# Attention to 32 memories and a spatial gate on one core: loads, written orders and the last output tile are rearranged

## The chip, the cores and the metric

The kernel runs on 1 core of one Trainium2 chip. The metric is the device time of one execution in microseconds (us). The kernel before was run three times; its time is the median of these.

## What is computed

There are 8 batches, 8 heads, 576 tokens (S), 64 columns per head (D), 32 memories (m), model width 512 and hidden width 1024. The reference, cut to what matters:

```
a     = softmax(phi, over tokens)              # 8 x 8 x 576 x 32
k_m   = einsum('bhsm,bhsd->bhmd', a, k);  v_m likewise from v
attn  = softmax(q @ k_m.T / sqrt(64))          # 576 x 32 per head
x     = attn @ v_m, heads side by side         # 576 x 512 per batch
h     = relu(x @ w_in);  u, v = halves of h    # 576 x 512 each
v_n   = (v - mean) / sqrt(var + 1e-6)          # over the 512 columns
v_s   = w_spatial @ v_n + b_spatial            # mixes the 576 tokens
out   = (u * v_s) @ w_out
```

w_in and w_out lie in memory as 64-bit floats, everything else as 32-bit floats.

## The kernel before

One core does the eight batches one after the other, in stages that overlap. x itself is never formed: the kernel multiplies the 32 memories of each head by w_in first (M = v_m @ w_in, the tiles `mh` and `ml`) and applies the attention weights (`ah`, `al`) to that. Matmuls on large tiles take a pair of rounded values, a high part (`mh`, `ah`, `vh`, `wth`, `gh`) and a low part (`ml`, `al`, `vl`, `wtl`, `gl`), and three products per pair. A low part is made by DVE (the vector engine, line 174), or by a matmul with minus the identity on PE (the matmul engine, line 162) and a copy on ACT (the scalar engine, line 172); the table `ON_VECTOR` says which.

Nothing is left to a scheduler. Each stage is a generator whose `yield`s cut it into steps, and every engine (PE, DVE, ACT, POOL, and SP, which issues all DMAs) executes its instructions in the order in which the written tokens call the steps. `START` is the order of the weights and of batch 0, `PLAN` that of each of the batches 1 to 6, `LAST` that of batch 7. A token is a letter, a number where the stage has several tiles, and one prime for each batch that the step is ahead; `*3` repeats it. The letters:

- Q: load q (batch 0 in one DMA, `q_all`, line 407; other batches in four DMAs of 128-byte pieces, `q_sb`, line 433) and transpose it (line 416 on PE, 442 on DVE).
- P: softmax weights over tokens. Load phi (303), maxima over rows (`half`, `mx`, 292 to 298), transpose on PE (`mt`, 311), maximum (`cm`, 314), spread (`cmb`, 317; `mb`, 320), subtract (322), exp (329), sums (`es`, again 292 to 298).
- K: load k and v (336), memories on PE (`kvm`, 348, 360), divide (`kmn`, 375; `vmn`, 384), transpose (388, 393; `kT`, 397).
- S: scores (460 for batch 0), their softmax (474 to 497) and its transpose `ta` (506) split into `ah`, `al` (509, 511). M: products with w_in (`mp`, 595), split into `mh` (604) and `ml`.
- V: the gate half of h by tiles of 128 tokens (`pv`, 627; bn at 651, normalize at 666, split at 669, 671). U: the other half (`pu`, 693). G: the mix over tokens (`ps`, 731) times u (`g`, 742), split (753, 755). O: the output product (`po`, 771), copied by ACT (777) and stored (780).
- D, E, L: two half loads of w_in (184, each 128 x 1024 words of 4 bytes) per token pair and their decoding to 32-bit floats (193, 195, 199, then the win step, 201). X: the same for w_out. W, T, B: load of w_spatial and of the bias (245 to 248), transposes (`wt`, 261, copied to `wth`, 272), bias row (282, the wsub step 284). Z: a matmul on the identity whose result nobody reads (`idle`, 791).

SP issues DMAs in the same order, and a DMA whose queue is full or whose tile is in use holds what stands behind it on SP. PSUM holds four single banks (`bank`) and two double ones (`banks`).

Of the kernel before, what the change touches and what calls it, by code (L numbers as in the profile page):

```python
# [23 lines left out]


START = """
    Q Z Q*3 Z P Q P*4 K Q P Q*2 P*2 K P Z P*6 K D1*2 K Z E0 K*3 D1 K Q*2 K D1 E1 E0 E1 P' Z K*2 W
    D0 P' S D0 Q S P' K Z E1 S T2 P' S E0 D0 T0 T2 Z S*3 T2 T0 S T0 D0 E0 T2 L0 E1 S*2 M1 T1 P' S
    T0 P' S B P' M1*2 T3 L1 S K' P' M1 L0 M1 K' S*2 P'*2 S T3 S M1 T3 S Q' S Q' S P' Z L1 S M1 K'
    S L0 L1 V0 T1 P' L0 V2 V0 V2 L1 T3 T1 V0 P' V0 M0 B M0 P'*2 V0 V2 K' T1 M0*2 T4 K' P'' V0 K'*2  # L30
    V0 T4 U2 Q' M0 K' Q' V2 X1 M0*2 V1 X1 V1 V3 T4*2 K' V2 V1 K' V2 V3 Q' U2 K' U2 K' X0*2 V3 P''
    U1*2 V1*2 U1 V2 P'' V3 U0 V1 X1 U0 P'' S U3 P'' U3 Q' U0 V4 U3 P'' V1 X1 P'' V4 S'*2 M0'*2 M1'
    S' G0 S'*2 G1*2 V4 S' M0' X0 M0' G1 V3 V4*2 V3 G0 X0 V3 P'' V4*2 P'' V4 G1 M1' X0 G0*2 M1' S'
    X1 G1 X0 G2*2 G0 X1 G3 M0' G3 X0 X1 X0 P'' M0' X1 G1 M1' S' G0*2 G1 G2*2 G0 M1' G0 G3 P'' G1
    Q'' G1 G3 O2 Q'' G3 M0' G2*2 O3 O1 S' K'' G3 G2 G3 M1' S'*2 M1' O3 S'*2 O1 O2 S' O2 O0 G2 O0
    K'' S'*2 G3 S' P'' S'*2 V1' O1 Q'' O0 G3 O0 O2 P'' O3 P'' G2 P'' V1' O1 O3 V1'*2
"""

PLAN = """
    Q' V4 U2 V1 K'*2 U0 Q' V0 K' V4 U3 U0 V0 U3 Q' P'' V2 V0 U1 U3 U1 K' V2 V0 V2 V3 K'*2 Q'' P''  # L40
    S' U1 S'*2 K' M0' V3 V4*2 M1' G0 V3*2 V2 M0' G1 M1' S'*2 M0' S' M1' G1 V2 V3 P'' Q'' G0 M1'
    P'' V2 M0' V4 G0 P'' M0' G1 V3*2 P'' G1 S' M0' G1 G0 P'' G0 S' G1 G2 G1*2 S' K''*2 G0 G1 G0 S'
    G2 S'*2 P'' G2 G0 P'' G3 G0 M1' G3 G2 S' G3 M1' G3 M0' O1 G3 O3 G2 S' P'' M1' O0 G3 P'' G2*2
    G3 S' O1 S' P'' O1 S' G2 S'*2 P'' O0 U2' O3 G3 Q'' O0 K''*2 O0 G2 V4' V1' G3 O4 O3 V4' O4 P'''
    U2' V1'*2 V0' O4 O3 V1' K'' V4' U0' O4 V0'*2 O2 V1' O1 V1' O2*2 P''' V2' O2
"""
# [12 lines left out]

# [812 lines left out]
```

## Time and profile before

| | |
|---|---|
| median of 3 runs | 415.53 us (414.77 to 415.92) |
| profiled execution, its own time | 414.95 us |
| its span, first to last instruction | 413.2 us |
| PE busy | 397.9 us (96%) |
| DVE busy | 283.7 us (69%) |
| ACT busy | 227.2 us (55%) |
| chain that ended last | PE 88%, DVE 4%, DMA 3%, ACT 2%, issue 2% |
| mean granted PE clock | 0.992 of full speed |

Busy time is summed over the span. The chain is followed back from the last instruction, at each step to what released it. Rows of the trace give a start, a duration, engine and line, the tiles as out<-in, and in brackets how long the engine idled before and what ended that; `x4` counts instructions in one row. Lines are those of the kernel before; in the changed kernel they are 3 higher up to the output copy and 7 higher behind it.

### The profile page before, as it was taken

What the parts mean: (1) busy time and instruction counts of PE and PEld (TensorE: products, weight loads), DVE (VectorE), ACT (ScalarE), POOL (GpSimd) and SP (SyncE); (2) the same over time, 40 slices, a digit from 0 to 9 for tenths busy, and PEclk for the clock granted to TensorE, in tenths of its full rate; (3) what the DMA queues carried; (4) which work ended last, traced back from release to release, by engine and by line L of the source; (5) the groups of instructions that cost most, each with busy time, mean ns of one, the idle gap of its engine ahead of it and who ended that gap; (6) DMA issues with size and microseconds to landing.
All of it is one profiled execution on the core that took longest, in us unless ns stands there. A gap on an engine that the chain in (4) does not pass through costs nothing.

```text
span 413.2 us, 9463 instructions
## 1 busy us (share of the span) xinstructions
PE 397.9 (96%) x3963; PEld 337.1 (82%) x3963; DVE 283.7 (69%) x542; ACT 227.2 (55%) x423; POOL 49.0 (12%) x131
## 2 busy tenths in 40 slices
PE   5778999999999999999999999999999999999996
PEld 3444688989798889989798888989798889989984
...
GB/s 293 387 379 252 96 239 254 51 42 132 252 81 27 135 144 230 0 52 154 290 12 25 135 143 229 0 68 137 248 54 37 68 27 1 2 76 27 0 2 127
DMA packets 85790, 50.70 MB, mean 123 GB/s; under 512 B 66226, under 2 KB 70322, under 8 KB 85748
## 3 DMA queue, kind: packets, MB, share of 16 engines
...
q8 instruction: 31, 0.51, 0.5%
...
## 4 chain that ended last, share of the span: by engine, by line
PE 88%; DVE 4%; DMA 3%; ACT 2%; issue 2%; SPq 0%; ACTq 0%; DVEq 0%
PE ps L731 28%; PE po L771 24%; PE pu L693 12%; PE pv L627 10%; PE kvm L348 4%; PE mp L595 2%; DMA w_rem<-in_moe_w_spatial_dram 2%; PE sc L529 2%; DMA q_all<-in_q_dram 1%; PE pv L636 1%; PE idle L791 1%; PE pv L637 1%; PE wt L261 1%; PE tq L416 1%; DVE win_sb L201 1%
## 5 line engine op out<-in xcount | busy, mean ns | idle before, releaser
L731 PE MATMUL ps<-wth,vh 128*128 128x288 f32 x256 | 56.9, 303 | 0.0
L731 PE MATMUL ps<-wth,vl 128*128 128x288 f32 x256 | 55.1, 297 | 0.0
L731 PE MATMUL ps<-wtl,vh 128*128 128x288 f32 x256 | 54.5, 294 | 0.0
L771 PE MATMUL po<-woh,gl 128*128 128x512 f32 x128 | 50.4, 394 | 0.0
L771 PE MATMUL po<-wol,gh 128*128 128x512 f32 x128 | 50.2, 392 | 0.0
L656 POOL TENSOR_SCALAR rs<-mv 128x1 f32<-128x1 f32 (+1 forms) x40 | 11.6, 290 | 324.9 <-DVE den L370 152.7
L771 PE MATMUL po<-woh,gh 128*128 128x512 f32 x128 | 50.0, 391 | 0.0
L651 DVE BATCH_NORM_STATS2 st<-vr 128x6 f32<-128x512 f32 (+1 forms) x40 | 27.0, 676 | 32.3 <-ACT vr L632 31.6
L731 PEld LDWEIGHTS ps<-wth,vh 128*128 128x128 f32 x256 | 41.2, 190 | 6.0 <-PE mp L595 5.9
L777 ACT COPY o<-po 128x512 f32<-128x512 f32 x36 | 20.8, 585 | 45.6 <-PE po L771 43.9
L731 PEld LDWEIGHTS ps<-wth,vl 128*128 128x128 f32 x256 | 41.0, 188 | 0.3 <-DVE vl L671 0.3
L731 PEld LDWEIGHTS ps<-wtl,vh 128*128 128x128 f32 x256 | 41.1, 188 | 0.0
L666 ACT ACTIVATE vr<-vr,sh,rs 128x512 f32<-128x512 f32 (+1 forms) x40 | 32.6, 817 | 4.6 <-POOL sh L661 3.8
L742 DVE TENSOR_TENSOR g<-u,ps 128x576 f32<-128x576 f32 x32 | 23.4, 747 | 10.8 <-PE ps L731 10.7
L771 PEld LDWEIGHTS po<-woh,gl 128*128 128x128 f32 x128 | 24.1, 188 | 5.3
L753 ACT CAST gh<-g 128x512 fp32r<-128x512 f32 x32 | 19.1, 617 | 16.7 <-DVE g L742 16.6
L671 DVE TENSOR_TENSOR vl<-vr,vh 128x512 fp32r<-128x512 f32 x32 | 21.6, 674 | 9.2 <-ACT vh L669 9.2
L771 PEld LDWEIGHTS po<-wol,gh 128*128 128x128 f32 x128 | 24.0, 188 | 4.7
L771 PEld LDWEIGHTS po<-woh,gh 128*128 128x128 f32 x128 | 24.0, 188 | 4.5
L693 PE MATMUL pu<-ah,mh 128*128 128x288 f32 x128 | 27.6, 297 | 0.0
L693 PE MATMUL pu<-al,mh 128*128 128x288 f32 x128 | 27.4, 296 | 0.0
L693 PE MATMUL pu<-ah,ml 128*128 128x288 f32 x128 | 27.3, 294 | 0.0
...
## 6 DMA issues: line engine op xcount, KB each, us to landing
...
```

The lines of the kernel that those rows point to most:

```text
L348: nc.tensor.matmul(kvm[r][32 * j : 32 * j + 32], phi_sb[halves[r], j, i, :], kv_sb[halves[r], j, :, i * D : (i + 1) * D], start=(i == 0), ...
L627: nc.tensor.matmul(pv, x[:, r, cs], m[:, r, DM:DFF], start=(n == 0), stop=(n == 5))
L651: nc.vector.bn_stats(st6, vr)
L656: nc.gpsimd.tensor_scalar_add(rs, mv[:, 1:2], 1e-6)
L666: nc.scalar.activation(vr, vr, AF.Identity, bias=sh, scale=rs)
L671: nc.vector.tensor_tensor(vl[:, st, :], vr, vh[:, st, :].bitcast(F32), op=ALU.subtract)
L693: nc.tensor.matmul(pu[:, hf, 0:HALF], m[:, r, cs], a[:, r, hf * HALF : (hf + 1) * HALF], start=(n == 0), stop=(n == 5),)
L731: nc.tensor.matmul(ps[:, hf, 0:HALF], a, w[:, hf * HALF : (hf + 1) * HALF], start=(n == 0), stop=(n == len(ops) - 1),)
L742: nc.vector.tensor_tensor(g.rearrange("p (a s) -> p a s", a=2), u[:, dt, :].rearrange("p (a s) -> p a s", a=2), ps[:, :, 0:HALF], op=ALU.mult,
L753: nc.scalar.copy(hi, x)
L771: nc.tensor.matmul(po, a, w, start=(n == 0), stop=(n == 11))
L777: nc.scalar.copy(o, po)
```

## The change

All three written orders are new. The parts of it that have a name:

- phi of batch 0 is loaded ahead of q (`P Q P` opens `START`).
- Five half loads of w_in, not four, are issued ahead of phi of batch 1; the other three follow w_spatial.
- q of batch 1 is split around v: k, two q loads, v, two q loads. One half of w_out is loaded ahead of phi of batch 2.
- There are seven idle matmuls, not eight.
- `ON_VECTOR` names other low parts: the counts (six `ml`, two `wtl`) are the same.
- The last output tile, now that of O3, is copied in two halves, by ACT and by DVE.

The diff, with the orders cut to their first lines:

```
 START = """
-    Q Z Q*3 Z P Q P*4 K Q P Q*2 P*2 K P Z P*6 K D1*2 K Z E0 K*3 D1 K Q*2 K D1 E1 E0 E1 P' Z K*2 W
-    D0 P' S D0 Q S P' K Z E1 S T2 P' S E0 D0 T0 T2 Z S*3 T2 T0 S T0 D0 E0 T2 L0 E1 S*2 M1 T1 P' S
...
+    P Q P Z P K*2 D1 P Q P*2 Q*2 P*2 Q P*3 Q P Z P Q D1 Q K E0 D1*2 P*2 K*2 Z K*2 E0 K Q*2 K E1
+    K*2 E0 Q D0 E1*2 K P' E0 Z S P'*2 S W S P' S Z S D0 Z P' T0 T2 S T0 P' S*2 D0 E1 T0 T2 D0 P'
...
 LAST = """
...
-    O1 O3 G2 O0 G2 O3 G3 O1 G3 O0*2 O4 O2 O4 O3 O1 O2*2 O3 O4 O2
...
+    G3*3 O1*3 G3 O2 O0 O2 G0 O4 O1 G3 O4 O0 O4 O0 O4 O3*3 O2 O3
 """
+
+FINAL = int(LAST.split()[-1][1])
...
-    E0 E1 L0 L1 X0 X0.sign X1 X1.sign ml001 ml011 ml100 ml101 ml110 ml111 wtl1 wtl4
+    E0 E1 L0 L1 X0 X0.sign X1 X1.sign ml000 ml001 ml010 ml101 ml110 ml111 wtl3 wtl4
...
         o = four.tile([P, DM], F32, name="o")
-        nc.scalar.copy(o, po)
+        if b == B - 1 and st == FINAL:
+            nc.scalar.copy(o[:, 0:256], po[:, 0:256])
+            nc.vector.tensor_copy(o[:, 256:DM], po[:, 256:DM])
+        else:
+            nc.scalar.copy(o, po)
```

What it moves on the engines, at three places. First SP, the DMA queue's engine, from the first loads of w_in (`raw`) to q of batch 1; the rows above these are phi, q, k and v of batch 0. Before:

```order
L184 DMA raw<-in_moe_w_in_dram 128x1024 x4
L303 DMA phi_sb<-in_phi_dram 128x4x288
L245 DMA w_sb<-in_moe_w_spatial_dram 128x4x576
L246 DMA w_rem<-in_moe_w_spatial_dram 64x576
L248 DMA b_sb<-in_moe_b_spatial_dram 1x576 x2
L184 DMA raw<-in_moe_w_in_dram 128x1024 x4
L336 DMA kv_sb<-in_k_dram 128x4x576
L336 DMA kv_sb<-in_v_dram 128x4x576
L433 DMA q_sb<-in_q_dram 32x72x32 x4
```

Changed:

```order
L187 DMA raw<-in_moe_w_in_dram 128x1024 x5
L306 DMA phi_sb<-in_phi_dram 128x4x288
L248 DMA w_sb<-in_moe_w_spatial_dram 128x4x576
L249 DMA w_rem<-in_moe_w_spatial_dram 64x576
L251 DMA b_sb<-in_moe_b_spatial_dram 1x576 x2
L187 DMA raw<-in_moe_w_in_dram 128x1024 x3
L339 DMA kv_sb<-in_k_dram 128x4x576
L436 DMA q_sb<-in_q_dram 32x72x32 x2
L339 DMA kv_sb<-in_v_dram 128x4x576
L436 DMA q_sb<-in_q_dram 32x72x32 x2
```

A fifth `raw` precedes phi of batch 1 and all that follows it, and v of batch 1 now stands behind two of the four `q_sb` loads.

Second PE, around the first transposes of w_spatial (`wt`), where it also takes the transpose of the row maxima of batch 1 (`mt`). `mp` is M of batch 0, `ta` the transpose of its attention weights. Before, from the last of the first M products on:

```order
L595 MATMUL mp_1_0_415<-win_sb,vT 32x512
L595 MATMUL mp_1_1_416<-win_sb,vT 32x512
L261 MATMUL wt_425<-ident,w_sb 128x128 x4
L261 MATMUL wt_425<-ident,w_rem 128x64
L311 MATMUL mt_436<-ident,mx 128x128
L162 MATMUL mp_1_0_415<-mh,minus 128x512
L261 MATMUL wt_444<-ident,w_sb 128x128 x4
L261 MATMUL wt_444<-ident,w_rem 128x64
L506 MATMUL ta_459<-ident,sm_all 128x128 x3
L320 MATMUL mb_464<-ident,cmb 128x128
```

Changed, from the idle matmuls ahead of the first `wt` on:

```order
L798 MATMUL idle<-ident 128x512 x2
L264 MATMUL wt_381<-ident,w_sb 128x128 x4
L264 MATMUL wt_381<-ident,w_rem 128x64
L264 MATMUL wt_387<-ident,w_sb 128x128 x4
L264 MATMUL wt_387<-ident,w_rem 128x64
L314 MATMUL mt_395<-ident,mx 128x128
L165 MATMUL wt_381<-wth,minus 128x256
L165 MATMUL wt_381<-wth,minus 128x320
L598 MATMUL mp_1_0_421<-win_sb,vT 32x512
L598 MATMUL mp_1_1_422<-win_sb,vT 32x512
```

`mt` stood behind the low parts of `wth`, the M products and a third `wt`; it now follows the second `wt` at once.

Third, the end of the program with the semaphores that each instruction waits for. SP before:

```order
L780 DMA out_dram<-o 128x512 [waits DMAHW0_49]
L780 DMA out_dram<-o 128x512 [waits DMAHW1_49,Activation_49]
L782 DMA out_dram<-o 64x512 [waits DMAHW2_49]
L783 DMA out_dram<-o 64x512 [waits DMAHW3_49]
L780 DMA out_dram<-o 128x512 [waits DMAHW4_49,Activation_49]
```

SP changed:

```order
L787 DMA out_dram<-o 128x512 [waits DMAHW0_49,Activation_49]
L789 DMA out_dram<-o 64x512 [waits DMAHW1_49,Activation_49]
L790 DMA out_dram<-o 64x512 [waits DMAHW2_49]
L787 DMA out_dram<-o 128x512 [waits DMAHW3_49]
L787 DMA out_dram<-o 128x512 [waits DMAHW4_49,DVE_49]
```

DVE changed, its last instructions (before, it had no part in the output tile):

```order
L745 TENSOR_TENSOR g<-u,ps_3_4894 128x576 [waits DVE_49,PE_49]
L758 TENSOR_TENSOR gl<-g,gh 128x512 [waits Activation_49]
L758 TENSOR_TENSOR grl<-g,grh 128x64
L758 TENSOR_TENSOR grl<-g,grh 128x64 [waits Activation_49]
L782 COPY o<-po_3_5038 128x256 [waits DMAHW4_49,DMAHW3_49,DMAHW7_49,DMAHW0_49,Activation_49]
```

The last store waited for ACT and now waits for DVE, and DVE's half of the copy waits for ACT, not for PE.

## Rows read from the trace of the kernel before

**Rows 1.** The page: busy us of each engine, share of the span, instructions.

```profile
PE 397.9 (96%) x3963; PEld 337.1 (82%) x3963; DVE 283.7 (69%) x542; ACT 227.2 (55%) x423; POOL 49.0 (12%) x131
```

**Rows 2.** Windows: stretch, length, busy PE, PEld, DVE, ACT, POOL, PE clock, DMA share, GB/s.

```profile
20.00:30.00 10.00, 7.31 (x161) 4.73 (x159) 7.57 (x10) 5.75 (x10) 0.00 (x0) 0.87 1.04 380
27.30:34.20 6.90, 6.37 (x28) 2.94 (x29) 4.20 (x8) 4.67 (x8) 0.00 (x0) 0.51 1.04 393
48.00:91.00 43.00, 42.87 (x326) 37.22 (x327) 40.66 (x71) 30.94 (x55) 5.34 (x14) 1.00 0.51 146
50.00:400.00 350.00, 349.93 (x3325) 306.33 (x3326) 251.91 (x488) 194.28 (x371) 44.78 (x116) 1.00 0.37 101
```

**Rows 3.** Timeline, 0 to 20 us: start, us, engine, line, operation, idle before.

```profile
6.27 1.97 PE L416 MATMUL tq<-ident,q_all 128*128 128x128 f32 x8 [2.20 <-DMA q_all<-in_q_dram]
...
7.89 0.69 DVE L292 TENSOR_TENSOR half<-phi_sb 128x512 f32<-128x512 f32 x1 [7.89 <-DMA phi_sb<-in_phi_dram]
...
16.50 1.14 ACT L193 ACTIVATE raw<-raw 128x1024 int32<-128x1024 uint32 x1 [2.11 <-DMA raw<-in_moe_w_in_dram]
...
17.55 0.60 ACT L375 ACTIVATE kmn<-kvm,den 128x128 f32<-128x128 f32 x2
```

**Rows 4.** Timeline, 20 to 30 us.

```profile
20.14 0.35 ACT L397 COPY kT<-tk 128x256 f32<-128x256 f32 x1
...
22.10 0.69 DVE L292 TENSOR_TENSOR half<-phi_sb 128x512 f32<-128x512 f32 x1 [0.60 <-DMA phi_sb<-in_phi_dram]
...
25.56 0.69 DVE L476 TENSOR_TENSOR sm_all<-sc,rmx_all 128x512 f32<-128x512 f32 x1
...
25.64 0.66 PE L261 MATMUL wt<-ident,w_sb 128*128 128x128 f32 x4 [1.45 <-DMA w_sb<-in_moe_w_spatial_dram]
...
26.86 10.57 SPq L433 DMA_DIRECT2D q_sb<-in_q_dram  x2
```

**Rows 5.** Timeline, 30 to 51 us.

```profile
30.05 1.35 DVE L486 TENSOR_REDUCE rsum_all<-sm_all 128x36 f32<-128x1152 f32 x1 [1.54 <-ACT sm_all L483]
...
35.01 0.29 DVE L314 TENSOR_REDUCE cm<-mt 128x2 f32<-128x128 f32 x1 [1.90 <-PE mt L311]
...
41.76 0.90 DVE L511 TENSOR_TENSOR al<-ta,ah 128x384 fp32r<-128x384 f32 x1
...
43.17 2.34 DVE L201 SCALAR_TENSOR_TENSOR win_sb<-raw 128x1024 int32<-128x1024 int32 x2
...
47.79 0.29 DVE L298 TENSOR_TENSOR es<-es,phi_sb 128x128 f32<-128x128 f32 x1
...
49.90 0.53 PE L693 MATMUL pu<-ah,mh 128*128 128x288 f32 x2
```

**Rows 6.** Timeline, 69 to 72 and 89 to 92 us.

```profile
69.83 0.75 DVE L742 TENSOR_TENSOR g<-u,ps 128x576 f32<-128x576 f32 x1
...
90.00 0.76 DVE L574 TENSOR_TENSOR al<-aT,ah 128x576 fp32r<-128x576 f32 x1 [0.17 <-ACT ah L572]
...
90.74 0.39 PE L627 MATMUL pv<-ml,ah 128*128 128x512 f32 x1
...
90.97 0.39 PE L627 MATMUL pv<-mh,al 128*128 128x512 f32 x1
```

**Rows 7.** DVE by line and form, 0 to 60 us: busy us, mean ns.

```profile
L201 DVE SCALAR_TENSOR_TENSOR win_sb<-raw 128x1024 int32<-128x1024 int32 x4 | 4.7, 1212 | 0.0
...
L294 DVE TENSOR_TENSOR half<-half 128x256 f32<-128x256 f32 x5 | 2.1, 417 | 0.1
...
L174 DVE TENSOR_TENSOR ml<-mp,mh 128x512 fp32r<-128x512 f32 x2 | 1.3, 660 | 0.0
...
L284 DVE TENSOR_TENSOR ws<-b_sb,ws 1x576 fp32r<-1x576 f32 x1 | 0.8, 755 | 0.0
```

**Rows 8.** Timeline, the last matmul and the last copy.

```profile
409.05 0.40 PE L771 MATMUL po<-woh,gl 128*128 128x512 f32 x1
409.52 0.58 ACT L777 COPY o<-po 128x512 f32<-128x512 f32 x1 [1.73 <-issue]
```

More of the change, by code (lines that the diff above doesn't have):

```diff
@@ L26 @@
 START = """
-    Q Z Q*3 Z P Q P*4 K Q P Q*2 P*2 K P Z P*6 K D1*2 K Z E0 K*3 D1 K Q*2 K D1 E1 E0 E1 P' Z K*2 W
-    D0 P' S D0 Q S P' K Z E1 S T2 P' S E0 D0 T0 T2 Z S*3 T2 T0 S T0 D0 E0 T2 L0 E1 S*2 M1 T1 P' S
-    T0 P' S B P' M1*2 T3 L1 S K' P' M1 L0 M1 K' S*2 P'*2 S T3 S M1 T3 S Q' S Q' S P' Z L1 S M1 K'
-    S L0 L1 V0 T1 P' L0 V2 V0 V2 L1 T3 T1 V0 P' V0 M0 B M0 P'*2 V0 V2 K' T1 M0*2 T4 K' P'' V0 K'*2
-    V0 T4 U2 Q' M0 K' Q' V2 X1 M0*2 V1 X1 V1 V3 T4*2 K' V2 V1 K' V2 V3 Q' U2 K' U2 K' X0*2 V3 P''
@@ L32 @@
[L32 to L36, printed above, removed]
+    P Q P Z P K*2 D1 P Q P*2 Q*2 P*2 Q P*3 Q P Z P Q D1 Q K E0 D1*2 P*2 K*2 Z K*2 E0 K Q*2 K E1
@@ new lines @@
+    K*2 E0 Q D0 E1*2 K P' E0 Z S P'*2 S W S P' S Z S D0 Z P' T0 T2 S T0 P' S*2 D0 E1 T0 T2 D0 P'
+    S*2 P' S B S M1 P' L0 T0 T2 T1 M1 T2 S L1 S P' M1 S M1 L0 M1 S L1 S*4 T3 K' M1 S T1 L1 S Q' M1
+    Z L0 L1 V2 L0 V2 V0 K' T1 P' V2 M0 P'*2 V0 M0 P' K' M0 P' V2 V0*2 M0 T1 K' M0 T4 Q' X1 T3 V1
+    M0 V2 V0 M0 U2 K' V2 T3 U2 P'' V1 X1 T4 T3 V3 V0 U1 Q'*2 K' V1 X0 T4 X0 S U2 U1 K' T4 V1 K' U3
+    K'*2 B U3 V2 V1 U1 V0 V1 U0*2 Q'*2 P'' V1 V3 K' X1 V3 U3 P'' V4 P'' V3 U0 X1 K' S' V4 S'*2 X0
+    K'' M1' Q'' M0' M1' G0 S'*2 M1' V3 V4 K'' V3 G1 S' M1' G1 V4 P'' G1 V4 M0' G0 M0' V3 P'' G0
@@ L37 @@
+    V4*2 X0 P'' V4 G1 X1 P'' X0 S' G1 M0' X0 X1 G0 X0 M1' G3 G0 X0 M1' X1 P'' G3 X1 G1 G3 M0' G1
+    G3 G0 G2 G1 G0 G2 P'' M0' G0 Q'' G1 M0' G0 G2*2 G3 O2 G2 O3 S' G2 S' G3 G2 P'' G3 O1 S' O3
+    S'*2 O2 G2 S' O2 O3 S' P'' S' P'' O1 O0*2 O1 S' G2 P'' O1 S' G3 M1' G3 U2' S'*2 O3 O0*2 P''
+    V1' Q'' O2 V1'*2 Q'' V1'
 """
 PLAN = """
-    Q' V4 U2 V1 K'*2 U0 Q' V0 K' V4 U3 U0 V0 U3 Q' P'' V2 V0 U1 U3 U1 K' V2 V0 V2 V3 K'*2 Q'' P''
-    S' U1 S'*2 K' M0' V3 V4*2 M1' G0 V3*2 V2 M0' G1 M1' S'*2 M0' S' M1' G1 V2 V3 P'' Q'' G0 M1'
@@ L42 @@
[L42 to L45, printed above, removed]
+    K' V4 V0 U2 V1 P'' U0 V4 Q' U0 Q'' K' U1 K' Q' U1 V0 P'' V2 U3*2 V0 V3 V0 V2 K' U3 K' S' U1 S'
+    K' M1' M0' V2 S'*2 V3 M1' V2 V3*2 V4 G0 V2 G1 S' V3 G0 S' M1' V3 V2 V4 V3 G1 V4 G1 S' M0'
@@ L46 @@
+    P''*2 M0' G1 S' G0*2 G3 G1 M1' M0' P'' Q'' G3 G0 G1 P'' S' G3 M0' M1' G1 G3 P'' M1' P'' M0'
+    K'' S' G1 M1' G2*2 G0 G2 G1 G0 S' G0 O3 S' P'' G2 G0 O1 G3 G2 G3 S' G2 G3 G2 S'*2 O0 M0' S' O1
+    U2' P'' O0 O3 O1 G3 P'' S'*2 P'' S' O0 O3 P''*2 O3 K''*2 V1' K'' O1 V4' V1' G3 V1' V4' O2*2
+    V4' O0 V1' O2 P''' G2 V0'*2 G2 O4 Q'' V1' U2' O4 U0' V0' O4 V1' V2' K''' Q'' O2 O4 K''
 """
 LAST = """
-    U2 V3 V0 V4 V0*2 U0 V2 V1 U1*2 V0 V3 U0 U1 V2 U3*2 V4 G0 V2 G0 G1*2 V2 V3 U3 V1 V2 V4*2 V3*3
@@ L50 @@
-    V2 G1 G0 V4 V3 G1*2 G0 G2 G0 G2 G0 G1 G3 G0 G1 O0 G1 G3 G2 G3*2 G0 G1 G3 G0 G2 O4 G3*2 O1 G2*3
-    O1 O3 G2 O0 G2 O3 G3 O1 G3 O0*2 O4 O2 O4 O3 O1 O2*2 O3 O4 O2
+    U2 V0 V2 V0 V4 V0 U0 V1 U3 U0 U3 V3 V2 U1 V0 U3 V4 U1 V3 V2 G0 V4 U1 V2*2 V4 V3 G0 G1*2 V3 V2
+    V3 V4 G1 G0 V3*2 G0*2 G1 G3 G0 G1 G3 G1 G2 G3 G2 G0 G2 G1*2 O2 G1 G2 O0 G2 G3 G2 V1 G2 G0 G2*2
+    G3*3 O1*3 G3 O2 O0 O2 G0 O4 O1 G3 O4 O0 O4 O0 O4 O3*3 O2 O3
 """
+FINAL = int(LAST.split()[-1][1])
 ON_VECTOR = set(
     """
-    E0 E1 L0 L1 X0 X0.sign X1 X1.sign ml001 ml011 ml100 ml101 ml110 ml111 wtl1 wtl4
+    E0 E1 L0 L1 X0 X0.sign X1 X1.sign ml000 ml001 ml010 ml101 ml110 ml111 wtl3 wtl4
```

## The prediction, made before the change was run

> **What bounds the kernel now.** The busy line of the page comes first [rows 1]: PE, the matmul engine, is busy for 397.9 us of a span of 413.2, so some 15 us are left that an order of work could win at all. The windows say where they lie [rows 2]. From 50 to 400 us PE is busy for 349.93 us of 350: it never waits there. All its gaps lie in the first 50 us and in the last few. In the gapless stretch the change leaves PE the same matmuls, so only three things can move the end: how much work PE has behind it when the gapless stretch begins, whether a new gap opens later, and what follows the last matmul. From 48 to 91 us DVE, the vector engine, is busy for 40.66 us of 43, so DVE decides for batch 0 how early PE's food is ready. The timeline of the first 50 us then shows what DVE itself waits for.
>
> The sum is made against the profiled execution, whose own time is 414.95 us, 1.75 more than its span. The median of the runs is 415.53, so 0.58 is added at the end. A measurement of this kernel can tell some 0.3% from no change, 1.25 us: under 414.3 counts as faster, over 416.8 as slower.
>
> **Part 1, phi ahead of q: nothing.** phi is half as large as q, so it lands first, and the maxima of batch 0 can start some 3 us before 7.89 [rows 3]. But `mt`, which takes their transpose, stands on PE behind the first transpose of q, which waited for q until 6.27 and now waits for both, until about 7.9. What is left of the gain, under 1 us at `kvm`, dies on ACT: the decode of w_in (16.50, ended 2.11 us of idling for its load) still stands ahead of `kmn` (17.55). The bytes ahead of the first half load of w_in are the same in sum, so the decode and `kmn` stay where they are. Bounds: 0 to 0.9 gained; I take 0, since the row of `kmn` follows the decode's at once.
>
> **Part 2, the fifth half load ahead of phi of batch 1: DVE is ahead by 2.0 us after it.** One half load is 128 x 1024 words of 4 bytes, 0.52 MB. The transfers are saturated here (380 GB/s from 20 to 30 us, DMA share 1.04 [rows 2]), so all that is queued behind it lands 0.52 MB / 380 GB/s = 1.4 us later: phi of batch 1 at 23.5 instead of 22.1, w_sb at 27.0 instead of 25.6 [rows 4]. The new DVE order puts the win step of the decoded half into the hole ahead of phi, then takes the same maxima. By the durations of the rows the last score subtraction ends at 28.15 (it was 25.56 + 0.69 = 26.25). So DVE is 1.9 us late there. This is the price.
>
> What it buys comes next. Of the two win steps behind the subtractions (1.21 us each [rows 7]) one is now done in that hole, and the other fills time in which DVE used to idle: `rsum` waited 1.54 us for the exponentials [rows 5]. Then the order pays: `cm` waited 1.90 us for `mt` on PE, because `mt` stood behind the low parts of `wth`, the first M products at half clock and another weight transpose. Now it stands ahead of all of these and `cm` is done before `rsum`, at 29.6 against 30.05: 0.45 us early. From there the steps up to the third `al` are the same but for the lost wait, for `cm` itself (0.29) and for the last maximum (put at 0.29, as the `es` step of its shape), which lie behind: 0.45 + 1.90 + 0.29 + 0.29 = 2.9 early, `al` ends at 39.8 instead of 42.66. The wins, the gate's bn and the `es` sums follow; the wsub step (0.755 [rows 7]) is moved behind them, so `es` ends 2.9 + 0.76 - 0.16 = 3.5 us early, at 44.6 (it was 48.08). The 0.16 is a wait that my walk puts at the bn behind the gate's relu. PE, which waits on just these tiles, begins its gapless stretch (`pu` at 49.90 [rows 5]) early by as much.
>
> **Part 3, what batch 0 takes back: 1.5 us of 3.5.** DVE has no slack from here to 91 us, so each step that the new order puts earlier on it costs its duration. Up to the first `g` (69.83 [rows 6]) these are wsub, 0.755, and one more low part of M of batch 1, 0.66 [rows 7]: 3.5 - 1.42 = 2.1. Up to the last `al` of batch 1 (90.00, for which the sixth matmul of `pv` at 90.97 is just in time) they are wsub, one `half` of 128 x 256 (0.417), one sum (0.29) and two `grl` of 128 x 64, put at 0.2 each by the 0.29 of 128 x 128: 3.5 - 1.86 = 1.6; but there PE has done half a u tile more, six matmuls of 288 columns at 288/512 of the 0.23 us between the starts of the two `pv` of 512 [rows 6], 0.8 us: 2.4. The smaller decides: about 2.0 us gained. I read PE's own side as the check: its list up to the first `pu` is as long, less one idle matmul. A loose walk, in which each releaser costs what it cost before, gives 2.1 there.
>
> Bounds: at most 3.0 (all of `al`'s lead is kept), at least 0.
>
> **Part 4, the low parts on DVE or on PE: nothing of its own.** Six `ml` and two `wtl` are on DVE before and now; only which ones. One low part of batch 0 leaves PE and one of batch 1 goes there: each is one matmul of 512 columns, so PE's sum is the same.
>
> **Part 5, the order of batches 1 to 7: nothing.** PE's matmuls are equal and it has no gap to lose [rows 2]. I set DVE's work against PE's need, token by token, with the durations of the rows: the least slack in a body is 3.1 us before, 5.0 after. On SP the stores of out and the q loads now stand ahead of v, but v is issued some 14 us ahead of its use. Batch 7 has some 0.2 us of slack at the last gate tile and at the last `g`, as before. Cover that fails there costs what is late, 1 us or so.
>
> **Part 6, the last tile in two halves: +0.2.** Before, one ACT copy of 512 columns (0.58) stands between the last matmul and the store [rows 8]. In the built order the DVE half waits for ACT, and the last store for DVE: the halves run one after the other. ACT's copy of 256 columns took 0.35 (`kT` [rows 4]), the nearest DVE step on 128 x 256 takes 0.417 [rows 7]: 0.77 without a pause between them, so +0.2. The bound on the other side, both at once, is 0.42 - 0.58 = -0.2. No row shows two engines reading one bank together. The Trainium skill, "PSUM — Partial Sum Buffer", section "PSUM bank collisions raise a hardware error", says that two engines may not access one bank in the same partitions at the same time, disjoint columns included; by that rule a split by columns can only be serial, as the built order has it, and splitting costs instead of saving.
>
> **The sum:** -2.0 + 0.2 = -1.8: 413.15 for the profiled execution, **413.7** on the median.
>
> **The rivals.**
> - *B, a new wait eats the lead.* The v load of batch 1 was issued ahead of the q loads; now two of these stand ahead of it, and SP was held for 10.57 us by the first two [rows 4]. v is then issued near 26.9 + 10.6 = 37.5 or later, and its 1152 KB at 380 GB/s land from about 41.2; the `kvm` that reads them comes at about 43.5 in my walk, behind the first gate tiles that need the third `al`. That is 2.3 us of slack in an estimate which is off by as much. If it fails, the lead of 2.0 goes first: 415.5 and no measurable change. The DMA share of 1.04 and 1.04 in the windows from 20 to 34 us speaks for it; the share of 0.51 from 48 us on [rows 2] says that the queue runs empty soon after, against.
> - *C, the clock (the slower side).* PE ran at half its clock, 0.51 granted in the window of 27.3 to 34.2 us, with 6.37 us busy of 6.9 [rows 2]; from 20 to 30 us it was busy for 7.31 us of ten. It cost 0.5 x 6.9 = 3.4 us of PE's time, most of it under DVE's cover. The new order has an emptier PE ahead of w_sb's transposes, 1.4 us longer. If the fall comes 10 us later, in the dense stretch, nothing covers it: 413.7 + 3.4 = 417.1. It decides from the point where the low stretch begins after about 40 us. Against it: the mean clock of 50 to 400 us is 1.00, so a PE that works without gaps did not lose it once.
> - *D, the whole lead is kept,* since PE does other work where DVE repays: -3.0 + 0.2, 412.7; without the serial tail 412.3.
>
> The Trainium skill, "TensorE: Matmul & The Clock Gate", section "HAM oscillation — how this bites in real kernels", says that a wait for DMA lets the clock fall and that the next dense part then starts slow; the fall at 27.3, behind 1.45 us of waiting for w_sb [rows 4], agrees. By it alone the fall stays with that wait, ahead of the dense stretch, and C would get half its chance.
>
> **How the numbers follow.** Forecast A, 413.7, 0.48; its own range is 412.9 to 414.4. B, 415.5 (414.3 to 416.7), 0.25. C, 417.1, 0.14. D, 412.5, 0.13. Faster: nearly all of A (0.44) and D, 0.56. Same: the rest of A and nearly all of B, 0.28. Slower: C and a little of B, 0.16. The range takes in D's centre and B whole: 412.0 to 416.9 leaves out a tenth or so on the slow side and a few hundredths on the fast one.
>
> **What would show it.** phi and w_sb of batch 1 land 1.4 us later; `cm` no longer waits for `mt`; `es` of batch 1 ends near 44.6; the first `pu` starts 2 to 3 us before 49.9; at the first `g` some 2 us are left, and they last to the end; behind the last matmul two copies stand one after the other, 0.8 us. Wrong: a `kvm` of batch 1 that ends its wait on v; a low clock after 40 us; PE under 349 of 350 us from 50 to 400; a lead that is there at 50 us and gone at 91.

## The result, and the profile after

| | before | changed |
|---|---|---|
| median of 4 runs | 415.26 us | 410.85 us (409.96 to 411.28) |
| ratio, 95% interval | | 0.9903 (0.9882 to 0.9923) |
| span of the profiled execution | 413.2 us | 408.8 us |
| mean granted PE clock of it | 0.992 | 0.994 |

The change makes the kernel faster by 4.4 us, where 1.8 had been forecast, and the time lies under the range given. The 415.26 are four runs; 80 later runs of the kernel before, beside the experiments, have a median of 414.7, against which the change gains 3.9. The busy line of the page of the changed kernel, against [rows 1]:

```profile
PE 392.5 (96%) x3961; PEld 335.0 (82%) x3961; DVE 287.9 (70%) x543; ACT 229.9 (56%) x423; POOL 47.6 (12%) x131
```

PE is busy for 5.4 us less with the same matmuls but for one idle step, which is two of them. Part of this is clock, as the windows of the changed kernel show (columns as in [rows 2]):

```profile
28.50:31.70 3.20, 3.20 (x22) 1.23 (x22) 2.56 (x5) 2.98 (x6) 0.00 (x0) 0.50 1.04 390
50.00:400.00 350.00, 350.00 (x3331) 306.60 (x3330) 252.79 (x483) 196.17 (x369) 42.87 (x114) 1.00 0.36 98
```

The stretch at the lower level, 1.2 GHz, is a little over 3.2 us here and was 6.9 [rows 2]; from 50 to 400 us PE is as full as before, by its busy time. The timeline of the changed kernel tells the steps up to the gapless stretch (columns as in [rows 3]):

```profile
13.84 2.22 PE L351 MATMUL kvm<-kv_sb,phi_sb 64*32 64x128 f32 x143 [1.21 <-DMA kv_sb<-in_v_dram]
...
22.73 0.69 DVE L295 TENSOR_TENSOR half<-phi_sb 128x512 f32<-128x512 f32 x1 [0.21 <-DMA phi_sb<-in_phi_dram]
...
26.38 0.69 DVE L479 TENSOR_TENSOR sm_all<-sc,rmx_all 128x512 f32<-128x512 f32 x1
...
26.55 0.66 PE L264 MATMUL wt<-ident,w_sb 128*128 128x128 f32 x4 [1.40 <-DMA w_sb<-in_moe_w_spatial_dram]
...
29.04 0.29 DVE L317 TENSOR_REDUCE cm<-mt 128x2 f32<-128x128 f32 x1 [0.84 <-PE mt L314]
29.25 1.34 DVE L489 TENSOR_REDUCE rsum_all<-sm_all 128x36 f32<-128x1152 f32 x1
...
37.56 1.65 DVE L514 TENSOR_TENSOR al<-ta,ah 128x384 fp32r<-128x384 f32 x2
...
42.91 2.21 PE L351 MATMUL kvm<-kv_sb,phi_sb 64*32 64x128 f32 x143
...
43.84 0.29 DVE L301 TENSOR_TENSOR es<-es,phi_sb 128x128 f32<-128x128 f32 x1
...
48.57 0.42 PE L696 MATMUL pu<-ah,mh 128*128 128x288 f32 x2 [0.50 <-DVE qT L445]
...
67.45 0.75 DVE L745 TENSOR_TENSOR g<-u,ps 128x576 f32<-128x576 f32 x1
...
87.73 0.76 DVE L577 TENSOR_TENSOR al<-aT,ah 128x576 fp32r<-128x576 f32 x1
...
404.45 0.40 PE L774 MATMUL po<-woh,gl 128*128 128x512 f32 x1
404.93 0.37 ACT L781 COPY o<-po 128x256 f32<-128x256 f32 x1 [2.21 <-PE po L774]
405.33 0.42 DVE L782 COPY o<-po 128x256 f32<-128x256 f32 x1 [7.74 <-ACT o L781]
```

The reader is to hold these against [rows 4 to 6] and [rows 8]. phi and w_sb land later (22.73 against 22.10, 26.55 against 25.64); the wait of `cm` for `mt` falls from 1.90 to 0.84 us and lies ahead of `rsum`; the third `al` ends at 39.21 (37.56 + 1.65) against 42.66, the sums `es` at 44.13 against 48.08. DVE is then 3.95 us ahead, 2.38 at the first `g`, 2.27 at the last `al` of batch 1. But the last matmul starts 4.60 us earlier. So PE won a further stretch of time after 92 us, where by its busy time there was nothing to win.

**A measure of this: the lead.** Each matmul shape gets its usual distance from start to next start (the median over all compared kernels, idle matmuls left out). The lead of a kernel at a time is the work, so counted, that the kernel before has still to start then, less the work that this one has.

| lead over the profiled execution of before, us | 48 | 100 | 205 | 310 | 360 | 400 |
|---|---|---|---|---|---|---|
| changed kernel | 2.97 | 2.78 | 3.54 | 4.12 | 4.45 | 4.58 |

2.8 us are there at 100 us, 1.8 more come in the bodies of batches 1 to 7, and from the start of the last `po` the changed kernel takes 4.37 us where before took 4.12: 2.8 + 1.8 - 0.25 = 4.35, which is the difference of the spans.

### The profile page after: what moved, and what is told of

The parts are those of the page before. It is cut to its first block, busy times and chain, and to the rows that moved or that the text cites. A ratio compares the mean times of both kernels' runs of the same rounds, so it can differ in the third digit from the quotient of the medians.

```text
span 408.8 us, 9476 instructions
## 1 busy us (share of the span) xinstructions
PE 392.5 (96%) x3961; PEld 335.0 (82%) x3961; DVE 287.9 (70%) x543; ACT 229.9 (56%) x423; POOL 47.6 (12%) x131
## 4 chain that ended last, share of the span: by engine, by line
PE 88%; DMA 5%; DVE 4%; ACT 1%; issue 1%; SPq 0%; ACTq 0%
PE ps L734 29%; PE po L774 24%; PE pu L696 12%; PE pv L630 10%; PE kvm L351 4%; PE mp L598 3%; DMA kv_sb<-in_v_dram 3%; DMA w_sb<-in_moe_w_spatial_dram 2%; PE sc L532 2%; PE pv L639 1%; PE pv L640 1%; ACT raw L202 1%; PE wt L264 0%; DVE ml L177 0%; PE tk L391 0%
## 5 line engine op out<-in xcount | busy, mean ns | idle before, releaser
L659 POOL TENSOR_SCALAR rs<-mv 128x1 f32<-128x1 f32 (+1 forms) x40 | 9.2, 229 | 322.1 <-DVE mv L656 313.6
L635 ACT ACTIVATE vr<-pv 128x512 f32<-128x512 f32 x32 | 19.2, 600 | 23.2 <-PE pv L630 23.0
## 6 DMA issues: line engine op xcount, KB each, us to landing
raw<-in_moe_w_in_dram SPq DMA_DIRECT2D x8, 512.0 KB, 11.4
```

Source lines behind the costliest of these rows:

```text
L635: nc.scalar.activation(vr, pv, AF.Relu)
```

## Experiments

The texts on record give the theories numbers and say what each expects. Theory 1 is that there are two separate gains, 2.8 us by the order of weights and batch 0 (`START`) and 1.8 by the bodies' orders (`PLAN`, `LAST`). Against it stood, in the order in which the runs took them up: that all of it comes from `START`; that the addresses of tiles do, which follow from the order in which `START` asks for them; that the shorter low clock does; and, inside `START`, which of its moves counts: the fifth half load, or `mt` ahead of the low parts and M products, last (theory 5) with the order of ACT that goes with it. All ratios are to the kernel before on the same chip, with 95% intervals. The lead column pairs are at 100 and at 360 us.

| run | ratio | median us | lead |
|---|---|---|---|
| e1_start_only | 0.9924 (0.9901 to 0.9946) | 411.29 | 2.96, 3.58 |
| e2_plan_only | 0.9997 (0.9980 to 1.0014) | 414.41 | 0.08, 0.46 |
| e3_q_first | 0.9897 (0.9876 to 0.9919) | 410.46 | 2.78, 4.24 |
| e4_four_halves | 0.9925 (0.9898 to 0.9953) | 411.19 | 3.93, 4.69 |
| e5_four_same_tiles | 0.9916 (0.9885 to 0.9947) | 410.42 | 3.05, 4.69 |
| e6_mt_late | 0.9943 (0.9924 to 0.9963) | 412.27 | -0.26, 1.38 |
| e7_aligned | 0.9910 (0.9886 to 0.9934) | 410.35 | 2.91, 4.24 |
| e8_best | 0.9928 (0.9904 to 0.9953) | 411.39 | 4.17, 5.38 |
| e9_before_tiles_moved | 0.9986 (0.9969 to 1.0003) | 414.20 | 1.45, 1.61 |
| e10_after_tiles_back | 0.9929 (0.9914 to 0.9945) | 412.10 | 3.18, 4.24 |
| e11_mt_early | 0.9994 (0.9980 to 1.0009) | 414.75 | 2.17, 2.07 |
| e12_three_parts | 0.9969 (0.9957 to 0.9981) | 413.44 | 0.61, 1.38 |
| e13_mt_and_act | 1.0021 (1.0002 to 1.0041) | 415.90 | -3.09, -2.99 |
| e14_four_parts | 0.9991 (0.9972 to 1.0010) | 414.56 | -1.71, -0.46 |

A lead is of one profiled execution, with the clock that it happened to be granted; the section on the clock says why this matters.

### START alone, PLAN alone

e1 has the changed `START` and `ON_VECTOR` with the old `PLAN`, `LAST` and single copy; e2 the reverse.

```diff
 e1: START, ON_VECTOR of the changed kernel
 e2: PLAN, LAST, split copy of the changed kernel
```

> The changed START and table of low parts with the PLAN and LAST of before and one copy of the last tile. Theory 1 (two separate gains: 2.8 us of lead gathered before 92 us by START, 1.8 us by PLAN and LAST, and 0.2 us lost at the split tile): 2.8 us below before, 412.5, with the waits of `po` for the bank that DVE's `vr` add holds back in three batches. Rival 2 (all of it comes from START, and the bodies only differ because another START hands them other banks): 4.6 below, 410.7. Rival 3 (START is worth the 2.0 us of the prediction and the rest lies elsewhere): 413.3.

> The START and table of before with the changed PLAN and LAST and the split copy. Theory 1: 1.8 - 0.2 = 1.6 us below before, 413.7, and the waits of `po` for `vr` gone. Rival 2: no gain, 0.2 slower, 415.5. Rival 3: 1 to 2.4 us below.

START alone gives 3.2 us (2.2 to 4.1 by the interval of the ratio), which fits theory 1 and neither rival. PLAN alone gives nothing that can be told from no change (at most 0.8), where theory 1 wanted 1.6; by time it's rival 2 that holds there. And e1 is 0.4 us behind the changed kernel, which is within the noise. So in the times START is most of the gain, and PLAN's part is not shown by them; it is in the traces. There the changed kernel's lead grows by 1.67 from 100 to 360 us and e1's by 0.62 only. PE's busy time cannot tell why. The waits of PEld, the loading of the stationary tile ahead of each matmul, can: PEld from 92 to 400 us in the kernel before (waiting line, what it waited for, us in total, times, longest):

```profile
PEld ps L731 <- PE mp L595: 5.0, 6, 0.8
...
PEld po L771 <- DVE vr L647: 1.3, 3, 0.4
PEld ps L731 <- DVE vl L671: 0.3, 1, 0.3
```

The first row is in every kernel alike. The second and third are not in the changed one, which has in their place:

```profile
PEld po L774 <- ACT vr L635: 1.2, 5, 0.3
```

e1 keeps the old wait, with the old PLAN:

```profile
PEld po L774 <- DVE vr L650: 1.3, 3, 0.4
```

One of the three waits in the timeline of the kernel before, engine PEld:

```profile
136.87 0.19 PEld L627 LDWEIGHTS pv<-mh,al 128*128 128x128 f32 x1
137.49 0.19 PEld L771 LDWEIGHTS po<-woh,grh 128*128 128x128 f32 x1 [0.43 <-DVE vr L647]
137.60 0.19 PEld L771 LDWEIGHTS po<-wol,grh 128*128 128x128 f32 x1
```

The first `po` of O4 needs the PSUM bank that V4's `pv` held, until DVE has read it for `vr`. Loads are 0.23 us apart here; this one comes 0.62 behind the last, 0.39 late, and the next 0.11 behind it, which wins 0.12 back: 0.27 us are lost. PE's row shows no gap, because a row of 512 columns lasts 0.39 us while starts are 0.23 apart. Three such waits are 0.8 us. The five waits for ACT in their place move the starts by some 0.05 each. The one wait on `vl` (0.3) is gone in e1 too. In lead from 100 to 360 us, PLAN is worth 1.05 with the changed START (1.67 against 0.62).

e2 has PLAN's gain at first (lead 1.15 at 310 us) and loses 0.7 of it at one place, in PEld's timeline:

```profile
321.25 0.19 PEld L629 LDWEIGHTS pv<-ml,ah 128*128 128x128 f32 x1 [1.03 <-issue]
```

e12, which also joins the old START's start to the new PLAN, has the same stall (0.85 us, at 319.95); the changed kernel doesn't. But it isn't this pair's alone: between 317 and 323 us, always at a `pv`, e14 with the same pair has 0.50 us, e3 with the changed START and PLAN 0.45, and e5, e9 and e10 have 0.2 to 0.3. The profile shows nothing that PE waited for. Its cause stays open, and by its lead e2 would end some 0.7 us earlier without it.

### phi first, and the fifth half load

```diff
 e3:
-    P Q P Z P K*2 D1
+    Q P P Z P K*2 D1
 e4:
-    K*2 E0 Q D0 E1*2 K P' E0 Z S P'*2 S W S P'
+    K*2 E0 Q E1*2 K P' E0 Z S P'*2 S W D0 S P'
 e5: e4, with the tile that D0 takes asked for at its old place
```

> The changed kernel with q_all issued ahead of phi of batch 0 again. The prediction put phi ahead of q at nothing: then 410.85, no change against the changed kernel. Theory 1 now says that `kvm` of batch 0, which ended 0.6 us earlier, frees phi's tile and so SP, and that the loads of phi and of w_spatial for batch 1 moved up by 0.6 us: then `kvm` starts at 14.4, phi of batch 1 and w_sb are issued at 16.8 and land 0.6 us later than in the changed kernel, and the time is 0.6 longer, 411.4.

> The changed kernel with four half loads of w_in ahead of phi of batch 1, the fifth behind w_spatial. In the changed kernel the chain that ended last runs through the landing of w_sb at 26.55. If the fifth half load only delays it (theory 1), phi lands at 21.3 and w_sb at 25.2, 1.4 us earlier, and up to 1.3 us more are gained: 409.6. Rival: DVE's own work from 22 to 30 us, or the fifth half landing late for its decoding at 30.4, takes the place of the wait: no gain, 410.85, or up to 1 us slower, 411.9.

> Four half loads ahead of phi of batch 1, as in the run before, but the SBUF tile `gh` is reserved at the place where the changed kernel first asks for it, so that all tiles lie where they lie in the changed kernel (`gh` at byte 123200 of a partition, not 137696). Theory: moving that load was worth 1.0 us of lead at 92 us (3.8 against 2.8) and was paid back because every output matmul with `gh` as weights starts 234 ns after the one before it and not 230; the address of `gh`, 32 bytes off a multiple of 64, is the cause. Then the pace is 230 again and the time 1.0 to 1.2 us below the changed kernel, 409.7. Rival: the pace of 234 comes from something else (the chip, the order of the loads): then 234 stays and 410.9.

q first again (e3) changes nothing in the end: `rsum` at 29.34 against 29.25, the same lead. (phi of batch 1 is issued 0.57 us later, at 16.74 against 16.17, and the first `wt` starts 0.26 later.) With four half loads ahead of phi (e4) w_sb comes 1.24 us earlier, at 25.31, and the lead at 100 us is 3.93, 1.15 more, or 1.02 more than e7, whose clock was as full as that of e4 from 20 us on.

```profile
25.31 0.66 PE L264 MATMUL wt<-ident,w_sb 128*128 128x128 f32 x4 [0.70 <-DMA w_sb<-in_moe_w_spatial_dram]
```

So the fifth load isn't what gains; it costs DVE a microsecond that the time doesn't show: e4 is no faster. A reason for that is in the page of e4, where all three products of `po` are slower than in the changed kernel (392, 392 and 393 ns):

```profile
L774 PE MATMUL po<-woh,gh 128*128 128x512 f32 x128 | 50.7, 396 | 0.0
L774 PE MATMUL po<-wol,gh 128*128 128x512 f32 x128 | 50.7, 396 | 0.0
L774 PE MATMUL po<-woh,gl 128*128 128x512 f32 x128 | 50.7, 396 | 0.0
```

The later half load moved the tile `gh` from byte 123200 to 137696 of each partition. The sums of these three rows are 0.5, 0.5 and 0.3 us over those of the changed kernel, 1.3 together, and the lead grows by 0.76 from 100 to 360 us where the changed kernel's grows by 1.67. e5 asks for the tile at the old place and gets 392, 392 and 394 ns back, but its time is no lower than the changed kernel's beyond the uncertainty. Its profiled execution ran at half clock from 33.8 to 37.2 us and shows a lead of 3.05, so whether four loads are better by the microsecond stays open.

### Addresses of tiles

e7 and e8 give four small tiles whole multiples of 64 bytes, so that the large ones behind them begin at such multiples; e8 has four half loads and the single copy besides. e9 and e10 ask for all tiles of the pool at the program's start, in the order of the other kernel.

```diff
 e7:
-        cm = one.tile([P, 2], F32, name="cm")
+        cm = one.tile([P, 16], F32, name="cm")[:, 0:2]
...
 e9, e10:
+    for entry in """q_sb:2304 mx:128 half:512 ...""".split():
+        tag, words = entry.split(":")
+        one.tile([P, int(words)], F32, tag=tag, name="place")
```

> The changed kernel with four small tiles (`cm`, `den`, `rmx`, `rsum`) made as large as a multiple of 64 bytes, so that `gl` and `vl` too begin at a multiple of 64 bytes; nothing else differs. Theory of addresses: the output matmuls with `gl` as weights go from 235 to 230 ns (144 of them, 0.7 us), the `ps` matmuls with `vl` gain 1 ns or so (256 of them, 0.2): 409.9 to 410.1. Rival: the pace has another cause: no change, 410.85.

> Four half loads ahead of phi of batch 1, all weight tiles at multiples of 64 bytes, and the last tile in one ACT copy. If the three add up: 1.0 + 0.8 + 0.2 = 2.0 us below the changed kernel, 408.8, with one copy of 0.58 us behind the last matmul in place of 0.37 + 0.42. Rival (addresses don't matter): 410.7; rival (a serial split costs nothing): 409.0.

> The kernel before with nothing changed but where its SBUF tiles lie: they are reserved ahead of all work in the order in which the changed kernel first asks for them, so that `vh` lies at byte 93952 of a partition and not at 104736, `gh` at 123200 and not 132416, and so on. Theory 4: part of what the changed START gains in the gapless stretch is a by-product of these places. The `ps` matmuls on `wth` with `vh` go from 141 to 139 ns and those on `wtl` with `vh` from 133 to 132 (256 of each): 0.8 us less, 413.9 against 414.65, with the same lead of 0 at 92 us. Rival: the pace follows the order of the instructions, and nothing changes: 414.65.

> The mirror image: the changed kernel with its tiles at the places of the kernel before. Theory 4: `ps` on `wth` with `vh` at 141 ns, 0.8 us more than the changed kernel, 411.5, with the lead of 2.8 us at 92 us kept. Rival: 410.7.

Multiples of 64 are not it: e7 has the time of the changed kernel and `po<-woh,gh` at 395 ns for 392, and in e8, with `gh` at 137792, a multiple of 64, `po` is as slow as in e4 (397 ns). Which addresses are slow, and why, stays open. Places explain little of the 4.4 us: the tiles moved in the kernel before (e9) give an unclear 0.6 us, the old places in the changed kernel (e10) take back 0.6 of the lead's growth (1.06 for 1.67). In time e10 is 1.2 us slower than the changed kernel, but five of its six runs had a lower mean clock than any of the four of that kernel. The rows of `ps<-wth,vh` follow the places: 303 ns before and in e10, 301 in the changed kernel and e9 (page of e9, then of e10):

```profile
L735 PE MATMUL ps<-wth,vh 128*128 128x288 f32 x256 | 56.4, 301 | 0.0
L738 PE MATMUL ps<-wth,vh 128*128 128x288 f32 x256 | 56.9, 303 | 0.0
```

Counted by the distances between starts from 92 to 400 us, as the lead is, this one shape takes 0.7 us less in the changed kernel than before and 0.6 less in e9, and e10 gives 0.6 of it back. e8 has the largest lead of all, 5.38, and a profiled time of 409.59, but its nine runs lie between 409.43 and 413.28: no version here beats the changed kernel by more than the measurement tells.

### Where `mt` stands, with and without the rest

e6 puts `mt`, `cm`, `cmb` and `mb` of batch 1 in the changed kernel back behind the low parts, M products and the third `wt`. e11 moves them ahead in the kernel before. e12 is e11 with the changed PLAN and LAST and the changed places of tiles. e13 and e14 are e11 and e12 with ACT's order of the changed kernel up to the first `ah` as well (the bias row ahead of `wtl`, `ah` ahead of `ml`).

```diff
 e6 (changed START):
-    T0 P' S*2 D0 E1 T0 T2 D0 P' S*2 P' S B S M1 P' L0 T0 T2 T1 M1 T2 S L1 S P' M1 S
+    T0 S S D0 E1 T0 T2 D0 S S S B S M1 L0 T0 T2 T1 P' M1 T2 P' S L1 P' S P' P' M1 S
 e11 (START before):
-    T2 P' S E0 D0 T0 T2 Z S*3 T2 T0 S T0 D0 E0 T2 L0 E1 S*2 M1 T1 P' S T0 P' S B P' M1*2
+    T2 P' S P' E0 D0 T0 P' T2 Z S S S T2 T0 S T0 D0 E0 E1 P' P' T2 L0 S S M1 P' T1 S T0 S B M1 M1
 e13 (on e11):
-    T2 Z S S S T2 T0 S T0 D0 E0
-    E1 P' P' T2 L0 S S M1 P' T1 S T0 S B M1 M1 T3 L1 S K' M1 L0
+    T2 S S S T2 T0 S D0 E0
+    E1 P' P' S S B L0 M1 P' T2 T0 T1 M1 T0 S S S L1 S K' L0 S M1 Z T3 M1 M1
```

> The changed kernel with `mt`, `cm`, `cmb` and `mb` of batch 1 put back to where they stood before the change: `mt` behind the first M products and the third `wt`. Theory 1 (the prediction's main term): `cm` waits some 1 to 1.9 us for `mt` again, the subtraction of phi moves from 32.7 to 35, and the lead at 92 us falls from 2.8 to about 0.8: 412.9. Rival: the gain comes from the rest of the order of START (win, exponentials, low parts on other engines), and `mt` is worth under 0.5: 411.3.

> The kernel before with one part of the change: the last maximum, `mt`, `cm`, `cmb` and `mb` of batch 1 move ahead of the first M products (two steps of ACT, a low part and a decode, move behind `cmb`); four half loads, q ahead of phi, PLAN and LAST stay. Theory 1: `cm` no longer waits 1.9 us for `mt`, the third `al` ends 2.0 to 2.5 us earlier (40.2 to 40.7 against 42.66), and the lead at 92 us is 1.5 to 2.5 us: 412.4 to 413.1. Rival (`mt` pays only together with the rest of the changed START): under 0.5 us, 414.2.

> The kernel before with three parts: the early `mt` of the run before, the tiles at the places of the changed kernel, and the changed PLAN and LAST; START stays as it was otherwise (four half loads ahead of phi of batch 1, q ahead of phi). If these three are the change: 2.0 + 0.8 + 0.9 = 3.7 us below before, 410.9, as the changed kernel. Rival (the rest of START matters, or the parts don't add up): 412 or more.

> The kernel before with the early `mt` of e11 and ACT's order of the changed kernel up to the first `ah`: the bias row and a decode fill the time in which ACT waited for PE's low parts, `ah` goes ahead of the low part and the second `mh` of M, one idle matmul moves behind. In e12 `cm` no longer waited for `mt`, but the first `al` waited 1.93 us for ACT's `ah`. Theory 5 (the gain needs both: `mt` early and ACT's queue in another order, since each alone only hands the wait on): `al` no longer waits for `ah` by more than 0.4 us, `es` ends by 45.3 with the clock low from 28 us (47.2 in e12), the lead at 92 us is 2.0 to 2.8 us in either state of the clock, and the time 412.3 to 412.9. Rival (the next wait is one step further down): `es` near 46.5, lead under 1.2, 413.8 or more.

> e13 with the tiles at the places of the changed kernel and the changed PLAN and LAST. If early `mt`, ACT's order, the places and PLAN are the change: 2.3 us from the front, 0.3 from the places, 1.0 from PLAN, less the 0.2 of the split tile and the stall of 0.9 us at 320 us that e2 and e12 showed with this pair of START and PLAN: 412.1; without that stall 411.2. Rival (they don't add up): 413.0 or more.

e6 loses the whole lead (-0.26 at 100 us). Its timeline has the old wait again, and a second one behind it:

```profile
33.41 0.29 DVE L317 TENSOR_REDUCE cm<-mt 128x2 f32<-128x128 f32 x1 [1.33 <-PE mt L314]
...
34.87 1.35 DVE L325 TENSOR_TENSOR phi_sb<-phi_sb,mb 128x1152 f32<-128x1152 f32 x1 [0.70 <-PE mb L323]
...
39.78 1.63 DVE L514 TENSOR_TENSOR al<-ta,ah 128x384 fp32r<-128x384 f32 x2
```

The third `al` ends at 41.41, not 39.21. In time it costs 1.4 us (412.27 against 410.85), less than the lead says, for its profiled execution had the low clock twice (27.7 to 31.1 and 37.9 to 44.8 us). So `mt`'s place is needed for a part of the gain: e6 is still 2.4 us below the kernel before. And it isn't sufficient: with `mt` early in the old order (e11) the time doesn't move. (The lead of 2.17 of e11 is that of an execution without low clock from 20 us on; its three runs of that kind have a median of 413.19 us, those of the kernel before 413.17.) The wait only changes hands. In e12 `cm` is done at 29.02, but the first `al` waits for ACT:

```profile
28.73 0.29 DVE L319 TENSOR_REDUCE cm<-mt 128x2 f32<-128x128 f32 x1
...
37.37 0.88 DVE L516 TENSOR_TENSOR al<-ta,ah 128x384 fp32r<-128x384 f32 x1 [1.93 <-ACT ah L514]
```

e12 with its three parts gains 1.3 us, not 3.7. With ACT's order too (e13) the first `al` is in time and the second late by more:

```profile
36.98 0.84 DVE L512 TENSOR_TENSOR al<-ta,ah 128x384 fp32r<-128x384 f32 x1
...
42.26 0.87 DVE L512 TENSOR_TENSOR al<-ta,ah 128x384 fp32r<-128x384 f32 x1 [4.44 <-ACT ah L510]
```

There the second `ah` stands behind `ml`, `mh` and a `wth` on ACT, and `wth` waits 2.84 us for a `wt` that PE, at half clock from 36.6 to 43.5 us, takes behind two idle matmuls (2.08 us); in the changed kernel the three `ah` run at 34.03 and 35.20 us, ahead of the next `wth`. e14 has the same wait (4.52 us) and 414.56 us, its rival's result. Theory 5 fell in the form in which it was built, but these two runs take over ACT's order only as far as the first `ah`: the lead is not one move's, and which set of moves is enough is not settled. The q loads split around v, the early half of w_out, the names in `ON_VECTOR` and the idle matmuls were not run by themselves.

### The clock, from the runs at hand

Each run lists its mean granted clock. Up to the last matmul, all low clock of the profiled executions lies in the first 45 us, and how much there is differs from run to run of one kernel. Two things blur the mean. In eleven of the sixteen profiles the lower level comes again behind the last matmul, where PE has nothing left to do (1.4 us in the changed kernel). And the clock's record begins only 9.3 to 14.0 us after the start; what lies ahead of it counts as full, but in every profile the transposes `tq` there come at about half the pace of those behind. In the changed kernel, whose record begins at 11.4 us:

```profile
7.74 1.11 PE L419 MATMUL tq<-ident,q_all 128*128 128x128 f32 x4 [3.67 <-DMA q_all<-in_q_dram]
...
12.02 0.60 PE L419 MATMUL tq<-ident,q_all 128*128 128x128 f32 x4
```

So PE works at the lower level there in all of them, and full clock below means from then on. The 80 runs of the kernel before beside the experiments, and 15 of the changed kernel, e3 and e7 (which have its START but for the first tokens and some tile sizes):

| mean clock | before: runs, median us | changed, e3, e7: runs, median us |
|---|---|---|
| 0.999 to 1.000 | 8, 413.17 | 2, 410.37 |
| 0.994 to 0.996 | 22, 414.63 | 10, 410.33 |
| 0.990 to 0.992 | 36, 414.74 | 2, 410.62 |
| 0.987 to 0.988 | 6, 415.85 | 1, 412.3 |
| 0.984 | 8, 416.12 | |

The old order pays 1.5 us for a little low clock, the changed one nothing that shows until there is more (its first and third groups are two runs each; with e1, e4, e5, e8 and e10, which keep most of its START, the first two groups are 3 runs at 410.59 and 25 at 410.63). e9, the old order at other places, was profiled at full clock: windows from 20 to 50 us, and `cm` in its timeline.

```profile
20.00:50.00 30.00, 23.92 (x412) 15.68 (x413) 26.36 (x42) 23.07 (x38) 2.58 (x6) 1.00 0.86 253
```

```profile
32.73 0.28 DVE L318 TENSOR_REDUCE cm<-mt 128x2 f32<-128x128 f32 x1
```

The first `wt` behind the wait for w_sb, in e9 and in e1:

```profile
25.66 0.66 PE L265 MATMUL wt<-ident,w_sb 128*128 128x128 f32 x4 [1.71 <-DMA w_sb<-in_moe_w_spatial_dram]
26.63 0.66 PE L264 MATMUL wt<-ident,w_sb 128*128 128x128 f32 x4 [1.86 <-DMA w_sb<-in_moe_w_spatial_dram]
```

`cm` doesn't wait in e9 at all, and comes 2.28 us before the 35.01 of [rows 5]: by this pair of executions the wait of 1.90 that the prediction saw removed was mostly the half clock's work on what stood ahead of `mt` (in e2, with the low clock from 25.6 to 32.5 us, it is 1.21). Without low clock the changed kernel is 2.8 us faster (413.17 - 410.37), with what is usual 4.3 (414.63 - 410.33). By the leads of e9 and e7, both at full clock, 1.5 of the 2.8 are START's (2.91 - 1.45); the rest is what the bodies gain, less the tail's 0.25.

## Why the prediction was right or wrong

- **Direction and place: right.** The end moves because DVE feeds PE earlier in the first 50 us; what was forecast there came within 1.1 us: the third `al` at 39.21 (39.8 said), `es` at 44.13 (44.6), the last score subtraction at 27.07 (28.15). Some signs failed. The loads came 0.63 and 0.91 us later, not 1.4; `cm` still waited 0.84 us for `mt`; and the first `pu` starts 1.33 us earlier and not 2 to 3, since PE takes other work first (its lead at 48 us is 2.97).
- **Part 1, phi ahead of q, nothing: right in time.** e3 shows it. The decode did not hold everything, though: the next loads are issued 0.57 us earlier than in e3.
- **Part 2, the price of the fifth load: too dear.** By itself it delays w_sb by 1.24 us (e4), near the 1.4 said, but with the rest of START w_sb came only 0.91 us later and phi 0.63, and the last subtraction 0.82, not 1.9. That it is a price and the order's rest the gain holds: e4 without it has 1.0 to 1.15 us more lead. Read as the place of `mt` alone, the gain is not shown: e6 loses a part without it, e11 gains nothing by it. And its size depended on a clock that I took as fixed; at full clock e9, the old order, waits for `mt` not at all.
- **Part 3, "the smaller decides: about 2.0 us gained": mis-sized.** It measured 2.8 between the two profiled executions. That 2.0 lies between this and the 1.5 of START at full clock is luck: the sum had no term for the clock. DVE was ahead by 3.95 at `es` and by 2.38 at the first `g` (2.1 said); up to the last `al` of batch 1 2.27, with the 0.8 reckoned for PE's own progress 3.1 (2.4 said). The smaller decided, near enough, but began 0.45 higher, by what Part 2 had overpriced.
- **Part 4, nothing of its own:** no row speaks against it, and it wasn't tried alone.
- **Part 5, "PE's matmuls are equal and it has no gap to lose": wrong, the step that failed.** Put at 0, it measured 1.8 us of lead from 100 to 400 us. From 92 us on it is 2.0: 0.8 are the three waits of `po` for a PSUM bank, 0.3 the wait on `vl`, 0.7 the pace of `ps<-wth,vh`, which follows the places of tiles (0.6 by e9 and by e10), and 0.2 the balance of smaller differences, the five waits for ACT among them. The waits of `po` went with PLAN, the places with START, and the wait on `vl` with either. A row of PE that overlaps the next start by 0.16 us hides a late start of that size whole, so a busy time of 349.93 of 350 was no proof. The waits of PEld, which stood in the same trace, were not read.
- **Part 6, +0.2: right.** The halves ran one after the other, 0.37 and 0.42 with 0.03 between them, for one of 0.58, and the tail is 0.25 longer. The Trainium skill, "PSUM — Partial Sum Buffer", section "PSUM bank collisions raise a hardware error", bars two engines from one bank in the same partitions; the trace agrees in so far as DVE's half ended its wait on ACT's, as the program's order asks; no run here has both at once.
- **Rival B, v late: did not come.** `kvm` of batch 1 at 42.91 waits for nothing.
- **Rival C, the clock: not as said, but its clause "most of it under DVE's cover" was the other mistake.** No profiled execution here has low clock between 45 us and the last matmul. In the old order it cost 1.5 us of the time by the table above, so it wasn't all covered; that the new order covers it is what the change gains beyond 2.8 us. The Trainium skill, "TensorE: Matmul & The Clock Gate", section "HAM oscillation — how this bites in real kernels", ties the low clock to the wait for a DMA ahead of it. Here the wait for w_sb was 1.45 us in the kernel before with the fall right behind it [rows 2, 4], 1.71 in e9 with no fall, 1.86 in e1 with a fall only at 33.6 us, 7 us later. By these, a wait of this length doesn't tell whether the clock falls. The case in that section of the Trainium skill has waits for DMA of some 3 to 5 us, which no run here has at that place.
- **Rival D, the whole lead kept (412.5):** nearest in time, though for other reasons.
- **The sum:** with the measured terms it is -2.8 - 1.8 + 0.25 = -4.35 for the profiled execution: 1.8 of the error is Part 5's and 0.8 Part 3's.
